# Placing row maxima without the way through DRAM, one group later, and borrowing maxima from the next work item

## The chip, the cores and the metric

The kernel runs on one core of one Trainium2 chip. The metric is device time in microseconds, the median of several executions. The engines of the core run their own instruction lists side by side and wait for one another through semaphores: TensorE (PE) multiplies, VectorE (DVE) takes maxima and small elementwise work, ScalarE (ACT) does the exponentials, GpSimd (POOL) elementwise work in the background, and SyncE (SP) issues nearly all DMAs.

## The reference, cut to what matters

One transformer block over 2048 rows of 512 columns: layer norm, attention with 32 heads of 16 dimensions over all 2048 keys, output projection and residual, then layer norm, a SiLU MLP of width 1792 and a second residual.

```
qkv = (layernorm(x) @ wqkv) -> q, k, v            # 32 heads, 16 wide
p = softmax(q k^T / 4);  o = p v
h = x + o @ wo
out = h + silu(layernorm(h) @ w1) @ w2
```

## The kernel before, in words

**Items and groups.** Attention is cut into 32 items: 4 blocks of 512 query rows times 8 sets of four heads. An item is cut into 16 groups, one for each 128 keys, so there are 512 groups (`g`); item `i` starts at group 16 `i`. In each group four score products (`scores`, `ps<-qs,ks`, one for each head) are made, ScalarE exponentiates each (`pt`), and two groups later `values` multiplies them with the values (`ps<-pt,va`, eight instructions a group, the last of it on TensorE).

**The maxima.** The softmax's row maxima are found by TensorE ahead of the scores: for each item 64 products (`maximum`, `ps<-ks,qs`: 2 row halves times 2 heads, 4 query tiles of 128 rows and 4 key blocks of 512), each reduced by VectorE (line 309, `mx`). When an item's 64 are there, `finish_max` takes the maximum over the key blocks (on VectorE if urgent, otherwise in six steps on GpSimd) and splits each into two 16-bit parts, `ns`, 128 partitions by 32. These parts have to lie as two more rows of each half of the *query stack* `qs` (partitions 64j + 48 and + 49 of half j), so that the score product subtracts the maximum by itself. No score of an item may run before its rows are there.

**Two ways to place them.** `place_max` turns `ns` on TensorE, copies the result (`mn`) and issues two DMAs `qs<-mn`. `place_far` turns 32 by 32 blocks on VectorE (`mt`, a transpose within VectorE), then issues four DMAs into the DRAM tile `md` one step later, and one step after that two DMAs from `md` into `qs`. A step is a group here. `found_maxima` takes the far way when the item starts more than FAR = 5 groups ahead (8 in an output item), and then waits CALM = 2 steps before the turn; otherwise `place_max` follows some steps later, and that group may hold one maximum fewer. The last item (31) always goes by `place_max`, in two pieces.

**Row halves.** Keys and queries of a head fill 64 of TensorE's 128 rows, so two products on different row halves run side by side, and two on the same half one after the other. The order alternates them. `todo[i, half]` holds the maxima of an item still to do in each half, 32 at first.

**Stages.** Groups 0 to 127 run attention alone, with three or so maxima a group. In items 8, 16 and 24 (`FIRSTS`) the attention output of the 512 rows just done is projected. From group 148, 276 and 404, for 112 groups each (`beside`), the MLP's products run beside attention, as halves too (`ps<-hts,w` and `ps<-w,gates`): six half products, four scores and four maxima a group. `beside_products` writes the order of such a group: even groups take the half products of row half 0 with scores of row half 1 for this group and the next, odd groups the other way round; of the maxima three go to the half of the scores and one to the other. How many maxima stand in the group is said by `maxima(g)`:

```
most = 4 - late_now + (64 + 4 * (g + LEAD) > at["done"])
```

with LEAD = 5: a fifth one, as long as the maxima done are behind the goal. `one_max` takes a maximum of the half asked for from the first item that has any left, and of the other half if that one has none; it turned to the next item only if that item's loads are due (`at["ready"]`) and the item's start is over 12 groups away.

**Queues.** All instructions stay in the order in which the program writes them, each engine its own. `soon(n, f)` puts `f` at the beginning of the n-th step from now. SP's queue holds the loads of keys and queries for the item four ahead (in the groups 6 to 13 of an item), the weights' loads, the small transfers of the softmax denominators, and the placing DMAs above.

Of the kernel before, what the change touches and what calls it, by code (L numbers as in the profile page):

```python
# [12 lines left out]
F16 = mybir.dt.float16  # L13
# [7 lines left out]
P = 128  # L21
# [9 lines left out]
KC = S // P  # L31
# [20 lines left out]
RING = 5  # L52

HEADS = [(0, 1), (0, 0), (1, 1), (1, 0)]
ITEMS = NB * H // 4
# [5 lines left out]
FIRSTS = 8, 16, 24  # L61


WAIT = 2
# [1 line left out]

JOINT = 2
MORE = 3, 3, 3, 3
FAR = 5
CALM = 2  # L70


# [1 line left out]

LOOK = 5

LEAD = 5

BEHIND = 4

# [11 lines left out]
def attention_mlp_kernel(ctx: ExitStack, tc: tile.TileContext, x, wqkv, wo, w1, w2, out):  # L92
    nc = tc.nc
    x = x.flatten_outer_dims()
# [14 lines left out]
    def pin(ins):  # L109
        tc.keep_in_program_order(ins)  # L110
# [11 lines left out]
    def dve(fn, *a, **k):  # L122
        pin(getattr(nc.vector, fn)(*a, **k))  # L123
# [4 lines left out]
    def dma(*a):  # L128
        pin(nc.sync.dma_start(*a))
# [27 lines left out]
    dram = ctx.enter_context(tc.tile_pool(name="dram", bufs=1, space=DRAM))  # L157
# [10 lines left out]
    def next_bank(kind):  # L168
        ring = banks[kind]
        ring.append(ring.pop(0))  # L170
        return ring[-1]
# [45 lines left out]
    dn = dram.tile([H, 4, 512], F32, name="dn")  # L217
    dr = dram.tile([H, 4, 512], F32, name="dr")

    md = dram.tile([ITEMS, 32, P], F16, name="md")  # L220

    wd = {kind: dram.tile([FC, P, 2, 512], F16, name=f"{kind}d") for kind in ("w1", "w2")}

    def statistics(rows, scale=1.0):
# [24 lines left out]
    ks, qs = [None] * RING, [None] * RING  # L249
# [26 lines left out]
    def head(g, k):  # L276

        i, c = divmod(g, KC)
        if i < LAST:
            return *HEADS[k], c  # L280
        return c // HALF, k % 2, c % HALF * 2 + k // 2
# [5 lines left out]
    def start_of(piece):  # L287
        i, a = piece
        return KC * i + HALF * (a or 0)

    mx, left = {}, {}
# [24 lines left out]
    def finish_max(piece, urgent):  # L316

        m4 = mx.pop(piece).rearrange("p j a q k -> p (j a q) k")
        rows = m4.shape[1]
        nm = small.tile([P, 16], F32, name="nm")[:, :rows]  # L320
        sign = 1.0
        if urgent:
            pin(nc.vector.tensor_reduce(nm, m4, axis=AX.X, op=ALU.max, negate=True))
        else:
            sign = -1.0
            m1, m2 = m4[:, :, :2], m4[:, :, 2:]
            for to, a, b in ((m2, m1, m2), (nm, m2[:, :, 0], m2[:, :, 1])):

                pool("tensor_tensor", to, b, a, ALU.subtract)
                pool("tensor_scalar", to, to, 0.0, None, op0=ALU.max)  # L330
                pool("tensor_tensor", to, to, a, ALU.add)
        ns = small.tile([P, 32], F16, name="ns")[:, :2 * rows]
        high, rest = (ns.rearrange("p (j r a) -> p j r a", j=2, r=2)[:, :, r, :] for r in range(2))
        nm = nm.rearrange("p (j a) -> p j a", j=2)
        pool("tensor_scalar", nm, nm, sign / MX, None, op0=ALU.mult)
        pool("tensor_copy", high, nm)
        pool("tensor_tensor", rest, nm, high, ALU.subtract)
        split[piece] = ns
# [7 lines left out]
    def place_far(piece):  # L346

        i, _ = piece
        mt = small.tile([P, 32], F16, name="mt")
        dve("transpose", mt, split.pop(piece))  # L350

        def out():
            for b in range(4):
                dma(md[i, :, 32 * b:32 * b + 32], mt[32 * b:32 * b + 32, :])

        def back():
            for j in range(2):
                dma(qs[i % RING][64 * j + 48:64 * j + 50].rearrange("r a n -> r (a n)"),
                    md[i, 16 * j:16 * j + 16, :].rearrange("(r q) n -> r (q n)", r=2))
            placed.add(piece)  # L360

        if at["attention"]:
            soon(1, out)
            soon(2, back)
        else:
            out()
            back()

    def place_max(piece):

# [8 lines left out]
        def out():  # L379
            for j in range(2):  # L380
# [8 lines left out]
    todo = {(i, j): sorted(((i, kb, qt, a, j) for kb in range(4) for a in range(2) for qt in range(4)),  # L389
                           key=lambda t: (t[1], t[3]) if i < 2 else t[3])  # L390
            for i in range(ITEMS) for j in range(2)}
    END = 64 * ITEMS
    at = {"item": 0, "done": 0, "half": 0, "step": 0, "due": 0, "attention": False, "group": None, "ready": 0, "next": 0, "blocks": True}
    agenda, late = {}, {}

    def soon(steps, fn, *a):

        agenda.setdefault(at["step"] + steps, []).append((fn, a))
# [11 lines left out]
    def next_item():  # L410
        while at["item"] < ITEMS and not (todo[at["item"], 0] or todo[at["item"], 1]):
            at["item"] += 1
        return at["item"]

    def found_maxima(piece):
        g = at["group"]
        output = g is not None and g // KC in FIRSTS
        if g is None or piece[1] is None and start_of(piece) - g > FAR + 3 * output:
            soon(WAIT + 1 if g is None else CALM, place_far, piece)
            finish_max(piece, g is not None and g > FIRSTS[0] * KC)  # L420
            return
        late.setdefault(at["step"] + (1 if output else WAIT), []).append(piece)
        unfinished.append(piece)
        found_at["step"] = at["step"]

    def one_max(half=None, n=None):

        i = next_item()
        if i == ITEMS:
            return  # L430
        if half is None:
            half = at["half"]
            at["half"] = 1 - half
        if at["blocks"]:

            i = min(range(2), key=lambda n: (todo[n, half] or todo[n, 1 - half] or [(n, KC)])[0][1])
        elif not todo[i, half] and 64 * (i + 2) <= at["ready"] and KC * i - at["next"] > 12:

            i += 1
        half = half if todo[i, half] else 1 - half  # L440
        maximum(*todo[i, half].pop(0), next_bank("sm") if n is None else n)
# [23 lines left out]
    def singles(n):  # L465
        for _ in range(n):
            one_max()
# [298 lines left out]
    for b in range(NB):  # L766
# [7 lines left out]
        for n, (kind, k) in enumerate(units + vs if b else units):  # L774
# [3 lines left out]
            if b + 1 < NB:  # L778
                rows = xts[b + 1]
# [76 lines left out]
    for g in range(1, NG // 2):  # L856
        for m, (b, key) in enumerate([(b, 1) for b in range(NB)] + [(b, 0) for b in range(NB)]):
# [3 lines left out]
            n = 8 * g + m - 12  # L861
# [340 lines left out]
    def beside_products(g, n):  # L1202

        if not current:
            count, share, of, end = chains.pop(0)
            current.update(count=count, share=share, of=of, end=end, half=[0, 0], open=[], gone=0)
        side = g % 2
        heads = [(x, k) for x in (g - side, g - side + 1) for k in range(4) if head(x, k)[1] != side]
        i, found, left = next_item(), [0, 0], [0, 0]
        if i < ITEMS:  # L1210
            left = [len(todo[i, j]) for j in range(2)]
        count = current["count"] - current["half"][0] if side == 0 else current["half"][0] - current["half"][1]
        count = min(current["share"], count)
        for _ in range(min(n, sum(left))):
            j = 1 - side
            if 4 + found[j] > count + found[side] or found[j] == left[j]:
                j = side
            if found[j] == left[j]:
                j = 1 - j
            found[j] += 1  # L1220
        other = [("score", of) for of in heads]
        for m in range(found[1 - side]):
            other.insert(2 * m if m < 3 else len(other), ("max", 1 - side))
        same = [("half", side)] * count + [("max", side)] * found[side]
        last = max(m for m, step in enumerate(other) if step[0] == "score")
        if last < count - 1:
            other[last:last] = [("none", 0)] * (count - 1 - last)
        for m in range(max(len(other), len(same))):
            for kind, x in same[m:m + 1] + other[m:m + 1]:
                if kind == "score":  # L1230
                    weigh = scores(*x)
                    if current.get("fence", True) is None:
                        current["fence"] = weigh()
                    else:
                        weigh()
                elif kind == "max":
                    one_max(x)
                elif kind == "half":
                    half_product(x)
                    if m == count - 1:  # L1240
                        current["fence"] = None
                        if current["half"][1] == current["count"]:
                            current["end"](space[:, 3, :])
                            current.clear()
# [132 lines left out]
    def maxima(g):  # L1377
# [4 lines left out]
        if g in beside:  # L1382
            at["due"] = 0
            most = 4 - late_now + (64 + 4 * (g + LEAD) > at["done"])
            return max(0, min(most, ready - at["done"]))
# [22 lines left out]
    for g in range(groups):  # L1408
        tick()
        i, c = divmod(g, KC)  # L1410
# [15 lines left out]
        if i in FIRSTS:  # L1426
            b, n = i // 8 - 1, c - OUTPUT
# [23 lines left out]
        n = maxima(g)  # L1451
# [3 lines left out]
        else:  # L1455
            half = 1 - head(g, g % 2)[1]
            j = next_item()
# [59 lines left out]
```

## Time and profile before

| | us |
|---|---|
| median of 3 runs | 1571.74 (1571.65 to 1571.79) |
| the profiled execution | 1571.37 |
| its span, from the first instruction to the last | 1569.6 |
| TensorE busy | 1553.5 |
| VectorE busy | 1377.7 |
| ScalarE busy | 1233.6 |
| GpSimd busy | 552.7 |

The granted TensorE clock was 1.000 over the span. In rows of the profile "a<-b,c" says that tile a is written from b and c; "x8" is the count of instructions merged into a row; the first number of a timeline row is its start after the span's start in us, the second the time it took. "SPq" is an issue of a DMA on SP's queue: the time is that of the issue, not of the transfer.

### The profile page before, as it was taken

What the parts mean: (1) busy time and instruction counts of PE and PEld (TensorE: products, weight loads), DVE (VectorE), ACT (ScalarE), POOL (GpSimd) and SP (SyncE); (2) the same over time, 40 slices, a digit from 0 to 9 for tenths busy, and PEclk for the clock granted to TensorE, in tenths of its full rate; (3) what the DMA queues carried; (4) which work ended last, traced back from release to release, by engine and by line L of the source; (5) the groups of instructions that cost most, each with busy time, mean ns of one, the idle gap of its engine ahead of it and who ended that gap; (6) DMA issues with size and microseconds to landing.
All of it is one profiled execution on the core that took longest, in us unless ns stands there. A gap on an engine that the chain in (4) does not pass through costs nothing.

```text
span 1569.6 us, 31094 instructions
## 1 busy us (share of the span) xinstructions
PE 1553.5 (99%) x11484; PEld 501.1 (32%) x11484; DVE 1377.7 (88%) x2216; ACT 1233.6 (79%) x2404; POOL 552.7 (35%) x759
## 2 busy tenths in 40 slices
PE   9999999999999999999999999999999999999999
PEld 6433322222222333333322333333322333332354
DVE  7999999999999999999999999999999999993322
ACT  6545799999977889888768998888868889888532
POOL 6643544445532344311142444311142544211100
PEclk9999999999999999999999999999999999999999
DMA  6667523333334022345423112444432221335332
GB/s 218 172 173 228 141 78 101 90 108 94 118 86 100 20 61 61 89 137 145 141 71 92 43 44 60 123 142 128 124 93 70 58 56 49 94 106 164 103 88 74
DMA packets 136209, 162.50 MB, mean 104 GB/s; under 512 B 43152, under 2 KB 80080, under 8 KB 136056
## 3 DMA queue, kind: packets, MB, share of 16 engines
q1 hardware_dynamic: 131304, 151.99, 34.8%
q10 hardware_dynamic: 4752, 8.52, 2.0%
q8 instruction: 90, 1.47, 0.4%
q14 instruction: 63, 0.52, 0.1%
HBM read 126.70 MB, written 24.85 MB: 97 GB/s over the span
## 4 chain that ended last, share of the span: by engine, by line
PE 87%; DVE 9%; ACT 2%; issue 1%; POOL 0%; DMA 0%; POOLq 0%; ACTq 0%; DVEq 0%
PE ps L99 87%; DVE mx L309 6%; ACT pt L113 2%; DVE mx L307 1%; PE ps L102 1%; DVE st L123 0%; DVE w L123 0%; DVE pvs L123 0%; DVE ot L123 0%; DVE ks L123 0%; POOL wv_l L106 0%; DMA ks<-in_A_x_dram 0%; POOL rs L106 0%; ACT g L113 0%; DVE mv L123 0%
## 5 line engine op out<-in xcount | busy, mean ns | idle before, releaser
L309 DVE TENSOR_REDUCE mx<-ps 128x1 f32<-128x512 f32 x1842 | 1145.7, 682 | 61.5 <-PE ps L99 31.5
L113 ACT ACTIVATE pt<-ps 128x512 f32<-128x512 f32 x2048 | 1050.0, 607 | 187.0 <-PE ps L99 185.2
L99 PE MATMUL ps<-ks,qs 48*128 48x512 f16 x2048 | 672.0, 379 | 5.7 <-DVE mx L309 2.7
L99 PE MATMUL ps<-qs,ks 64*128 64x512 f16 x2048 | 639.7, 377 | 1.8 <-ACT pt L113 1.4
L99 PE MATMUL ps<-pt,va 128*17 128x512 f32 x4096 | 538.6, 598 | 0.6
L99 PE MATMUL ps<-hts,w 64*128 64x512 f16 (+2 forms) x1212 | 285.0, 372 | 1.8 <-ACT pt L113 1.8
L99 PE MATMUL ps<-w,gates 64*128 64x512 f16 x1008 | 245.6, 378 | 0.1
L99 PEld LDWEIGHTS <-ks 64*128 64x128 f16 x2048 | 177.0, 94 | 212.1 <-issue 169.2
L99 PEld LDWEIGHTS <-qs 48*128 48x128 f16 x2048 | 167.0, 94 | 70.9 <-issue 29.4
L99 PEld LDWEIGHTS <-w 64*128 64x128 f16 (+1 forms) x1212 | 101.9, 95 | 236.8 <-ACT pt L113 107.2
L106 POOL TENSOR_TENSOR ri<-rc,minus 128x16 f32<-128x16 f32 x31 | 90.7, 2926 | 240.0 <-DMA rc<-dn 240.0
L99 PEld LDWEIGHTS <-gates 64*128 64x128 f16 (+1 forms) x1152 | 95.1, 94 | 240.3 <-ACT pt L113 112.8
L99 PEld LDWEIGHTS ps<-pt,va 128*17 128x17 f32 x4096 | 68.2, 95 | 204.9 <-issue 197.0
L307 DVE TENSOR_REDUCE mx<-ps 128x2 f32<-128x1024 f32 x103 | 119.3, 1218 | 4.0 <-PE ps L99 3.5
L106 POOL TENSOR_SCALAR t<-t,factors 128x512 f32<-128x512 f32 x42 | 29.0, 692 | 214.8 <-ACT t L113 214.8
L113 ACT ACTIVATE g<-ps,factors 128x512 f32<-128x512 f32 x68 | 46.9, 690 | 42.7 <-PE ps L99 42.7
L106 POOL TENSOR_TENSOR ot<-ot,g 128x512 f32<-128x512 f32 x12 | 15.3, 1271 | 128.5 <-ACT g L113 128.5
L113 ACT ACTIVATE ks<-ps 128x512 f32<-128x512 f32 x30 | 17.9, 597 | 51.7 <-PE ps L99 46.3
L123 DVE SCALAR_TENSOR_TENSOR gh<-g,factors,gh 128x512 f16<-128x512 f32 x14 | 10.5, 752 | 52.1 <-ACT gh L113 52.1
L106 POOL TENSOR_TENSOR t<-t,g 128x512 f32<-128x512 f32 x42 | 53.7, 1279 | 3.5
L106 POOL TENSOR_TENSOR sl<-ks,sh 128x512 f16<-128x512 f32 x30 | 34.7, 1156 | 50.4 <-ACT sh L113 38.6
L106 POOL TENSOR_TENSOR gates<-t,gates 128x512 f16<-128x512 f32 x42 | 48.6, 1158 | 3.4
(160 smaller groups left out, 992.4 us busy)
## 6 DMA issues: line engine op xcount, KB each, us to landing
w<-w2d SPq DMA_DIRECT2D x182, 256.0 KB
ks<-kd SPq DMA_DIRECT2D x120, 192.0 KB
w<-w1d SPq DMA_DIRECT2D x56, 256.0 KB
ks<-in_B_w_dram ACTq DMA_DIRECT2D x28, 256.0 KB
w<-in_B_w_dram SPq DMA_DIRECT2D x28, 256.0 KB
qs<-qd SPq DMA_DIRECT2D x128, 48.0 KB
kd<-sh SPq DMA_DIRECT2D x16, 256.0 KB
qd<-sh SPq DMA_DIRECT2D x16, 256.0 KB
```

What stands on the lines that cost most here:

```text
L99: return tc.keep_in_program_order(nc.tensor.matmul(*a, **k))
L102: tc.keep_in_program_order(nc.tensor.transpose(*a))
L106: tc.keep_in_program_order(getattr(nc.gpsimd, op)(*a, **k))
L113: ins = getattr(nc.scalar, fn)(*a, **k)
L123: pin(getattr(nc.vector, fn)(*a, **k))
L307: pin(nc.vector.tensor_reduce(of, space[:, n:n + 2, :], axis=AX.X, op=ALU.max))
L309: pin(nc.vector.tensor_reduce(of[:, j:j + 1], space[:, n, :], axis=AX.X, op=ALU.max))
```

## The change

`place_far` no longer writes `mt` to DRAM and back: eight DMAs (four blocks times two halves) go from `mt` straight into the rows of `qs`, one step after the turn. The DRAM tile `md` is gone. FAR falls from 5 to 3, LEAD from 5 to 4, and in groups up to 128 the turn waits three steps in place of two. In the groups beside the MLP, `beside_products` counts the next item's maxima as well if they are ready, and `one_max` may take them (`borrow`) where the first item has none left in the half asked for.

```diff
-FAR = 5
+FAR = 3
...
-LEAD = 5
+LEAD = 4
...
-    md = dram.tile([ITEMS, 32, P], F16, name="md")
...
         def out():
-            for b in range(4):
-                dma(md[i, :, 32 * b:32 * b + 32], mt[32 * b:32 * b + 32, :])
-
-        def back():
             for j in range(2):
-                dma(qs[i % RING][64 * j + 48:64 * j + 50].rearrange("r a n -> r (a n)"),
-                    md[i, 16 * j:16 * j + 16, :].rearrange("(r q) n -> r (q n)", r=2))
+                rows = qs[i % RING][64 * j + 48:64 * j + 50].rearrange("r a (q b n) -> r (a q) b n", b=4, n=32)
+                for b in range(4):
+                    dma(rows[:, :, b, :], mt[32 * b + 16 * j:32 * b + 16 * j + 16, :])
             placed.add(piece)
 
         if at["attention"]:
             soon(1, out)
-            soon(2, back)
         else:
             out()
-            back()
...
-            soon(WAIT + 1 if g is None else CALM, place_far, piece)
+            soon(WAIT + 1 if g is None else CALM if g > FIRSTS[0] * KC else CALM + 1, place_far, piece)
...
-    def one_max(half=None, n=None):
+    def one_max(half=None, n=None, borrow=False):
...
-        elif not todo[i, half] and 64 * (i + 2) <= at["ready"] and KC * i - at["next"] > 12:
+        elif not todo[i, half] and 64 * (i + 2) <= at["ready"] and (borrow or KC * i - at["next"] > 12):
...
-            left = [len(todo[i, j]) for j in range(2)]
+            known = [i, i + 1] if 64 * (i + 2) <= at["ready"] else [i]
+            left = [sum(len(todo[m, j]) for m in known) for j in range(2)]
...
-                    one_max(x)
+                    one_max(x, borrow=True)
```

## The prediction

> **What bounds the kernel now.** I read the page first: the busy shares, the granted clock and the chain that ended last.
>
> ```profile
> span 1569.6 us, 31094 instructions
> ...
> PE 1553.5 (99%) x11484; PEld 501.1 (32%) x11484; DVE 1377.7 (88%) x2216; ACT 1233.6 (79%) x2404; POOL 552.7 (35%) x759
> ...
> PEclk9999999999999999999999999999999999999999
> ...
> PE 87%; DVE 9%; ACT 2%; issue 1%; POOL 0%; DMA 0%; POOLq 0%; ACTq 0%; DVEq 0%
> ```
>
> TensorE is busy 99% of the span at full clock and carries 87% of the chain; VectorE carries 9%. So a change gains where it shortens TensorE's own order or one of the stretches in which VectorE leads, and any idle stretch put into TensorE's order is lost in full: it has no slack to win it back.
>
> Next, TensorE's timeline. Each group ends in eight value products, one row "x8"; from one such row to the next is one group.
>
> ```profile
> 511.07 1.05 PE L99 MATMUL ps<-pt,va 128*17 128x512 f32 x8
> 514.16 1.05 PE L99 MATMUL ps<-pt,va 128*17 128x512 f32 x8
> 517.37 1.05 PE L99 MATMUL ps<-pt,va 128*17 128x512 f32 x8
> 520.17 1.06 PE L99 MATMUL ps<-pt,va 128*17 128x512 f32 x8
> 523.26 1.05 PE L99 MATMUL ps<-pt,va 128*17 128x512 f32 x8
> ...
> 553.03 1.05 PE L99 MATMUL ps<-pt,va 128*17 128x512 f32 x8
> 556.06 1.05 PE L99 MATMUL ps<-pt,va 128*17 128x512 f32 x8
> 558.87 1.05 PE L99 MATMUL ps<-pt,va 128*17 128x512 f32 x8
> 561.48 1.05 PE L99 MATMUL ps<-pt,va 128*17 128x512 f32 x8
> 564.09 1.05 PE L99 MATMUL ps<-pt,va 128*17 128x512 f32 x8
> ```
>
> Beside the MLP a steady group takes 2.61 us (561.48 to 564.09). The exceptions are what the change is about. The first five rows end the groups 154 to 158 and show that five maxima in a group instead of four make it 3.09 us (155, from 511.07 to 514.16); the chain there is VectorE's.
>
> ```profile
> 509.43 3.08 DVE mx L309 x5
> ```
>
> The group that ends with the row at 556.06 (170) takes 3.03 us and the next 2.81, with four maxima each.
>
> **The change, part by part.** I number groups by the scores they belong to (item = group / 16) and followed the planner's rules from group to group; under the old rules they give in each group the count of maxima that the trace shows.
>
> *Lead of four.* A group beside the MLP gets a fifth maximum while done < 64 + 4 (g + LEAD). Before group 148, 664 are done; the old goal there is 676, the new one 672. Each five-group wins one, so the old catch-up is 12 fives (148 to 160, but for 157, where the late rows cost one maximum), the new one eight (148 to 155). Groups 156, 158, 159 and 160 fall from five to four: 156 from 3.21 us (514.16 to 517.37) to about 2.8, VectorE still finishing its backlog, the others from 3.09 to 2.61. Item 10 is found in group 155, five ahead of its start at 160; that now is "far", so the turn on TensorE in 157 goes (2.80, from 517.37 to 520.17, to about 2.65). Together -2.0 us. In the second and third stretch the deficit at entry is five under either rule (both ends moved by four): no gain. The four maxima put off land in group 491, which has none now:
>
> ```profile
> 1417.14 1.05 PE L99 MATMUL ps<-pt,va 128*17 128x512 f32 x8
> 1419.95 1.05 PE L99 MATMUL ps<-pt,va 128*17 128x512 f32 x8
> 1422.55 1.05 PE L99 MATMUL ps<-pt,va 128*17 128x512 f32 x8
> ```
>
> Group 490 with four takes 2.81, 491 without 2.60: +0.2 us.
>
> *Borrowing from the next item.* Halves run in pairs. In group 170 the item has one maximum left for half 1 and three for half 0, where the order wants three and one, so equal halves follow each other unpaired:
>
> ```profile
> 554.88 0.59 PE L99 MATMUL ps<-hts,w 64*128 64x512 f16 x2
> 555.31 0.37 PE L99 MATMUL ps<-qs,ks 64*128 64x512 f16 x1
> 555.32 0.81 PE L99 MATMUL ps<-ks,qs 48*128 48x512 f16 x3
> ```
>
> That is (3.03 - 2.61) + (2.81 - 2.61) = 0.62 us, and the counting gives one such pair of groups in each of the three stretches (170, 282, 410; in the first, the new catch-up leaves no such remnant either). The missing half is now taken from the next item: -1.8 us. The price: in stretches two and three, five groups of 4:1 in turn leave the halves three apart, and the old lack evened this out. Borrowing keeps it: in group 283 only maxima of half 0 are left of item 18, three are taken, one of half 1 comes from item 19, and the last of item 18 comes at the end of 284, four groups ahead of its start at 288. The same holds for items 18 to 24 and 26 to 30: **twelve items complete four ahead** (six before). Items 11 to 16 complete five ahead.
>
> *One group later in the first part.* There GpSimd finishes the maxima and VectorE's turn waits for it:
>
> ```profile
> DVE mt L123 <- POOL ns L106: 2.6, 4, 1.0
> ```
>
> VectorE then is what TensorE waits for:
>
> ```profile
> 294.85 1.05 PE L99 MATMUL ps<-pt,va 128*17 128x512 f32 x8
> 297.80 1.05 PE L99 MATMUL ps<-pt,va 128*17 128x512 f32 x8
> 299.76 1.05 PE L99 MATMUL ps<-pt,va 128*17 128x512 f32 x8
> ```
>
> 2.95 us where a group takes 1.96. The turn one group (1.96 us) later finds its rows finished, since the longest wait was under 1 us: all of it goes, -2.6 us.
>
> *Straight to the stacks.* Before, six issues on SP: four of 32 pieces of 64 bytes to DRAM, and, after they landed, two back. Item 11:
>
> ```profile
> 560.20 0.20 DVE L123 STREAM_TRANSPOSE mt<-ns 128x32 f16<-128x32 f16 x1
> ...
> 560.43 1.69 SPq L129 DMA_DIRECT2D md<-mt  x4
> 562.16 0.43 SPq L129 DMA_DIRECT2D ks<-kd  x1
> 563.29 0.52 SPq L129 DMA_DIRECT2D qs<-md  x2
> ...
> 570.57 0.38 PE L99 MATMUL ps<-qs,ks 64*128 64x512 f16 x1
> ```
>
> The turn stands 0.28 us into group 172 (559.92, the end of the x8 row at 558.87), SP issues at once, the back copies are issued by 563.81, and item 11's first score runs at 570.57: over 5 us of cover. Now there are eight issues, all from SBUF to SBUF, 16 pieces of 64 bytes each, two partitions as target. What does such an issue cost on SP? Not traced; two bounds. From below the copies out of the same tile, 1.69 us for four, 0.42 each (0.46 from one to the next when they follow at median length). From above the other writers of those two rows, also SBUF to SBUF and in 16 pieces:
>
> ```profile
> L129 SPq DMA_DIRECT2D qs<-mn x12: 616/647/717, 476.5 to 1426.3; - x12
> ...
> 476.50 1.41 SPq L129 DMA_DIRECT2D qs<-mn  x2
> ```
>
> 0.65 us each, 1.41 for two. The target and piece count are theirs, so I take 0.70 us from issue to issue: eight make 5.6. Landing: 562.12 to 563.29, 1.17 us, the least; the most by
>
> ```profile
> 907.59 1.69 SPq L129 DMA_DIRECT2D md<-mt  x4
> 909.33 1.56 SPq L129 DMA_DIRECT2D ks<-kd  x1
> 912.03 0.52 SPq L129 DMA_DIRECT2D qs<-md  x2
> ```
>
> is 2.75 (909.28 to 912.03). I take 1.2, as the copies no longer write DRAM.
>
> The deadline of an item found four ahead: the turn is placed two groups after, at start - 2, done 0.48 us into it; the copies stand in SP's order one group later but SP is idle by then, as at 560.43. First score in its group: the second pair (570.34 and 570.57 in item 11), so two groups and 0.21, 5.43 us (two groups back is 565.14). That score is of row half 1, whose four copies are issued last. Rows are there at 0.5 + 5.6 + 1.2 = 7.3. **TensorE stands still for about 1.8 us at the start of each of the twelve items: +21.6 us.** Found five ahead, the deadline is 8.08: no stall, 0.8 to spare. Behind the copies on SP wait weight loads, which run groups ahead: nothing.
>
> Item 8, in the first part, is found in 121; with the extra group its copies also come behind one more load of SP's:
>
> ```profile
> 424.16 1.05 PE L99 MATMUL ps<-pt,va 128*17 128x512 f32 x8
> ...
> 426.52 0.41 SPq L129 DMA_DIRECT2D ks<-kd  x1
> 427.03 1.76 SPq L129 DMA_DIRECT2D md<-mt  x4
> 428.83 0.42 SPq L129 DMA_DIRECT2D qs<-qd  x1
> ```
>
> From 427.5, after that load: 427.5 + 5.6 + 1.2 = 434.3. Group 124 begins at 425.21; without VectorE's wait four groups of 1.96 end at 433.05, and the first score is of half 1: +1.2 us. Items 3 to 7 have twelve groups or more.
>
> **Sum:** -2.0 + 0.2 - 1.8 - 2.6 + 21.6 + 1.2 = +16.6. The profiled execution took 1571.37 us, 0.37 under the median shown; 1571.74 + 16.6 = 1588.3, rounded to 1588.
>
> The Trainium skill (DMA: Bandwidth & Descriptors, "Issuing engines are not separate DMA queues") says that the time a sequencer needs to start a DMA is usually small beside the DMA itself. By that rule, eight issues would cost little and the sum would be that of the first rival; the rows of qs<-mn and md<-mt speak against it, since two issues of 4 KB in all hold SP for 1.41 us and the landing behind them is of the same size.
>
> **Rivals.** *The issues are cheap* (the other side). At md<-mt's 0.46 us the rows land at 0.5 + 3.7 + 1.2 = 5.4, just in time: no stall, and item 8's goes too. 1571.74 - 6.2 = 1565.5. For it: same source tile, same piece of 64 bytes. Against: every SBUF-to-SBUF issue into those rows takes over 0.6. The sign turns at (0.52 + 5.43 - 1.7) / 8 = 0.53 us an issue, where twelve stalls of 0.52 us eat the 6.2.
>
> *The items complete five ahead after all*, because borrowing is held back by the loads that are ready, or halves even out. Then only item 8 waits: 1571.74 - 6.2 + 1.2 = 1566.7. Against: the next item's keys are loaded four items ahead, so nothing holds it back.
>
> *The copies land late*, 2.75 us as at 912.03: the stall is 3.4 us, twelve make 41, six five-ahead items wait 0.7 each, 4.2, and item 8 waits 2.8: 1571.74 + 41 + 4.2 - 6.2 + 2.8 = 1613.5. For it: one of the traced chains; against: the landing there was a write to DRAM beside a 192 KB load, and in the last two groups before an item no such load is issued.
>
> **Chances and range.** The forecast 0.70 (by itself 1581 to 1598: the issue 0.64 to 0.75, from the shortest and the longest qs<-mn and some 0.03 between two, the landing 1.1 to 1.5 in the mean); cheap issues 0.17; five ahead 0.06; late landing 0.07. The range takes in the first two rivals: 1565 to 1598. Within 0.2% (3.1 us), about what a measurement of this kernel can tell from no change, is 1568.6 to 1574.9: an issue near the turning point, 0.05, taken from cheap issues and the forecast. Faster 0.20, same 0.05, slower 0.75.
>
> **What will show it.** The row of qs<-mt: x216 or so, 600 ns or more each, eight in a row over 5 us. Waits of TensorE or its weight loads on a DMA qs<-mt, about 13 times and near 1.8 us; idle stretches at the starts of items 18 to 24 and 26 to 30, none at 11 to 16. The wait of mt on POOL gone; no fives after group 155; no 3.03 at 170, 282 and 410. An issue of qs<-mt under 0.5 us, or no TensorE wait on it, makes the prediction wrong.

## The result: 0.7% slower, and the profile after

| | before | changed |
|---|---|---|
| median, us | 1571.76 (1571.65 to 1571.90) | 1583.09 (1582.93 to 1583.44) |
| the profiled execution, us | 1571.37 | 1582.93 |
| its span, us | 1569.6 | 1581.1 |

The ratio is 1.0073, with a 95% interval of 1.0061 to 1.0085. The page after, busy shares and chain:

```profile
span 1581.1 us, 31233 instructions
...
PE 1552.2 (98%) x11483; PEld 500.1 (32%) x11483; DVE 1379.8 (87%) x2216; ACT 1233.4 (78%) x2404; POOL 554.1 (35%) x759
...
PE 74%; DVE 13%; SPq 4%; DMA 4%; ACT 2%; issue 2%; POOL 1%; DVEq 0%; POOLq 0%; ACTq 0%
```

TensorE's busy time fell by 1.3 us while the span grew by 11.5: the added time is idle, not work. New in the chain are SP's queue and DMAs, 4% each. A share of the chain is not a cost: SP's copies run beside TensorE's products for most of their time, and only the part that outlasts them lengthens the span (below). One item's beginning in the chain after, in order of time (item 21, start at group 336; the reductions `mx` are line 309 before and line 307 in this kernel):

```profile
994.82 0.22 issue
995.04 0.68 DVE mx L307
995.72 0.12 DVE mt L123
995.84 0.68 DVE mx L307
996.52 0.04 SPq L129
996.55 0.05 issue
996.61 0.66 SPq L129
997.27 0.05 issue
997.32 0.61 SPq L129
...
999.94 0.61 SPq L129
1000.55 0.04 issue
1000.59 1.63 DMA qs<-mt
1002.22 0.14 issue
1002.36 7.71 PE ps L99 x60
```

VectorE's turn is followed by SP issuing one copy after another, the last copy's issue and landing, and then TensorE. The same item in the timelines of SP and TensorE:

```profile
994.37 1.05 PE L99 MATMUL ps<-pt,va 128*17 128x512 f32 x8
...
995.87 5.33 SPq L129 DMA_DIRECT2D qs<-mt  x8
...
1000.62 0.39 PE L99 MATMUL ps<-w,gates 64*128 64x512 f16 x1
1000.62 0.39 PE L99 MATMUL ps<-ks,qs 48*128 48x512 f16 x1
1000.85 0.38 PE L99 MATMUL ps<-w,gates 64*128 64x512 f16 x1
1002.36 0.37 PE L99 MATMUL ps<-qs,ks 64*128 64x512 f16 x1 [1.14 <-DMA qs<-mt]
```

The group before last begins at 995.42, where the x8 row ends, and the copies 0.45 us into it. The first pair of the item's first group runs at 1000.62. The score belongs to the second, at 1000.85, and starts 1.51 us after that, when the eighth copy has landed: its issue ended at 1001.20, the chain puts the landing at 1002.22, and the score starts at 1002.36, 1.16 after the issue's end. The bracket, 1.14, is TensorE's idle time alone; before it the partner product at 1000.85 ran without the score beside it. The group is 1.50 us longer than before.

The ends of the value products also show how far ahead VectorE's turn stands: in the kernel before in the fourth group ahead of an item's start for items 11 to 16 and for the twelve items, in the changed kernel in the third for items 11 to 16 and in the second for the twelve.

The costs and gains of all groups, from the ends of their value products in the two profiles:

| where | predicted, us | measured, us |
|---|---|---|
| starts of items 18 to 24 and 26 to 30, twelve stalls | +21.6 | +17.3 (1.37 to 1.50 each) |
| start of item 8 | +1.2 | +0.9 |
| groups 39, 60, 103, 124 | -2.6 | -2.6 |
| first stretch, groups 153 to 164 | -2.0 | -2.1 |
| unmatched pairs, groups 170, 171, 282, 283, 410, 411 | -1.8 | -1.7 |
| end of the maxima, groups 484 to 494 | +0.2 | +0.2 |
| all groups | +16.6 | +11.8 |

The span grew by 11.5 and not 11.8, since what follows the last value product is 0.2 us shorter.

The waits of the changed kernel and the row of the tile behind them:

```profile
PE ps L99 <- DMA qs<-mt: 13.7, 13, 1.1
PEld L99 <- DMA qs<-mt: 10.2, 7, 1.7
```
```profile
L129 SPq DMA_DIRECT2D qs<-mt x224: 596/610/742, 117.9 to 1400.9; - x112
L123 DVE STREAM_TRANSPOSE mt<-ns x28: 200/202/202, 115.0 to 1395.9; 128x32 f16<-128x32 f16 x28
its engine sat idle before it (us, times) until:
who waited for it (us, times):
```

The 13 waits of the first line are the twelve items and item 8. VectorE's wait of 2.6 us for ns is gone (nothing stands under "until"), and TensorE's long groups with it; in the timeline after, the group that was 2.95 us has the length of its neighbours:

```profile
294.52 1.05 PE L99 MATMUL ps<-pt,va 128*17 128x512 f32 x8
296.48 1.05 PE L99 MATMUL ps<-pt,va 128*17 128x512 f32 x8
```

### The profile page after: what moved, and what is told of

The parts are those of the page before. It is cut to its first block, busy times and chain, and to the rows that moved or that the text cites. A ratio compares the mean times of both kernels' runs of the same rounds, so it can differ in the third digit from the quotient of the medians.

```text
span 1581.1 us, 31233 instructions
## 1 busy us (share of the span) xinstructions
PE 1552.2 (98%) x11483; PEld 500.1 (32%) x11483; DVE 1379.8 (87%) x2216; ACT 1233.4 (78%) x2404; POOL 554.1 (35%) x759
## 4 chain that ended last, share of the span: by engine, by line
PE 74%; DVE 13%; SPq 4%; DMA 4%; ACT 2%; issue 2%; POOL 1%; DVEq 0%; POOLq 0%; ACTq 0%
PE ps L99 74%; DVE mx L307 9%; SPq L129 4%; ACT pt L113 2%; DMA qs<-mt 1%; DVE mx L305 1%; DMA w<-w2d 1%; DVE st L123 1%; PE ps L102 0%; DVE w L123 0%; DMA va<-in_A_wqkv_dram 0%; DMA hts<-gates 0%; DMA ks<-in_A_x_dram 0%; DVE pvs L123 0%; DMA ks<-kd 0%
## 5 line engine op out<-in xcount | busy, mean ns | idle before, releaser
L106 POOL TENSOR_SCALAR nm<-nm 128x16 f32<-128x16 f32 (+1 forms) x42 | 10.8, 258 | 147.2 <-DVE nm L321 141.8
```

Source lines behind the costliest of these rows:

```text
L106: tc.keep_in_program_order(getattr(nc.gpsimd, op)(*a, **k))
```

## The experiments

The theory: the rows are late because SP issues eight copies one after the other, the first score needs the last four of them, and borrowing leaves only two groups for it. The rivals: copies from SBUF to SBUF or their landing are slow by themselves, whatever their order; a lead of four is too short by any way; something else in the change costs time.

### Half 1 first

```diff
-            for j in range(2):
+            for j in (1, 0):
```

> The changed kernel with the eight copies in another order: the four of row half 1 first, then those of half 0. Theory (SP's serial issue): the first score of an item belongs to half 1, and what makes it late is that its four copies stand fifth to eighth in a row of issues of 0.655 us. First in the row they land at 0.5 + 4 x 0.655 + 1.2 = 4.3 us after the group before last has begun, before the score's 5.43; half 0 is due one group (2.61 us) later at 8.0 and lands at 6.9. The twelve stalls of 1.45 us go: 1583.1 - 17.4 = 1565.7 us; item 8's wait of 0.9 stays, since there half 0 follows at once. Rival (the copies themselves, or their landing, are slow from SBUF to SBUF, or the lead of four is too short by any order): the stall stays or falls by under half, 1575 us or more.

Measured: 1565.58 us (1565.40 to 1566.19); ratio to before 0.9961 (0.9948 to 0.9975), so faster than both kernels. The same item in this kernel's timelines of VectorE, SP and TensorE:

```profile
991.17 0.20 DVE L123 STREAM_TRANSPOSE mt<-ns 128x32 f16<-128x32 f16 x1
...
991.40 5.33 SPq L129 DMA_DIRECT2D qs<-mt  x8
...
996.16 0.39 PE L99 MATMUL ps<-w,gates 64*128 64x512 f16 x1
996.16 0.39 PE L99 MATMUL ps<-ks,qs 48*128 48x512 f16 x1
996.39 0.38 PE L99 MATMUL ps<-w,gates 64*128 64x512 f16 x1
996.39 0.38 PE L99 MATMUL ps<-qs,ks 64*128 64x512 f16 x1
```

SP is held just as long, 5.33 us, and still issuing when the group begins at 996.16; the score at 996.39 does not wait, since its half is there. The eight issues are as slow as before and cost nothing now. All twelve stalls are gone; item 8 still waits, as there half 0 follows at once, but its first group is 0.64 us longer than before and not 0.9, as the expectation had it.

### One place earlier

```diff
-            for j in range(2):
+            for j, b in ((0, 0), (0, 1), (0, 2), (1, 0), (1, 1), (1, 2), (1, 3), (0, 3)):
                 rows = ...
-                for b in range(4):
-                    dma(rows[:, :, b, :], ...)
+                dma(rows[:, :, b, :], ...)
```

> The changed kernel with one copy of half 0 moved behind those of half 1, so that the last one the first score needs is the seventh in the row and not the eighth. Theory (serial issue): each place in the row is worth one issue, so the stall falls from 1.45 to 0.80 us in twelve items, and item 8's, which needs both halves at once, stays: 1583.1 - 12 x 0.655 = 1575.2 us. Rival (the time from the last issue to the landing is what is too long, whichever place): no change, 1583 us.

Measured: 1575.10 us (1574.71 to 1575.62), ratio 1.0021 (1.0012 to 1.0030). The twelve groups are 0.71 to 0.84 us longer than before the change, in place of 1.37 to 1.50: one place is one issue, 0.65 us. The time is set by the place in SP's row of issues. Item 8 did not quite stay: its first group is 0.66 longer than before, in place of 0.89.

### A lead of five

```diff
-LEAD = 4
+LEAD = 5
```

> The changed kernel with LEAD at 5 again, all else as changed (direct copies, half 0 first, borrowing). By the planner's rules all items then complete five groups ahead. Theory: the rows land at 7.1 us and are due at 8.0, so no item but the eighth waits: minus 12 x 1.45; four groups of the first stretch (156 to 159) hold five maxima again, plus 4 x 0.46: 1583.1 - 17.4 + 1.8 = 1567.5 us. Rival (borrowing or the direct copies cost something that doesn't hang on the lead): over 1571 us.

Measured: 1568.14 us (1567.96 to 1568.64), ratio 0.9978 (0.9969 to 0.9987); expected 1567.5. None of the twelve items waits. The five-groups of the first stretch are back (156 to 159, 3.1 to 3.2 us), and group 490 is 0.43 us longer than before: in TensorE's timeline its 15 half products, scores and maxima stand in ten places one after another, in eight before, so more of them run without a partner. The expectation left this cost out.

### The way through DRAM kept

The copies of the kernel before (`out` and `back` over `md`), all else as changed.

```diff
+            for b in range(4):
+                dma(md[i, :, 32 * b:32 * b + 32], mt[32 * b:32 * b + 32, :])
+
+        def back():
             for j in range(2):
-                rows = ...
...
+                dma(qs[i % RING][64 * j + 48:64 * j + 50].rearrange("r a n -> r (a n)"),
...
+            soon(2, back)
```

> The changed kernel with the rows going through DRAM as before (four issues out of 0.42 us, after their landing two back of 0.24), LEAD 4, FAR 3, borrowing and the later turn kept: twelve items still complete four ahead. Theory (serial issue): 0.5 + 1.7 + 1.2 + 0.5 + 1.2 = 5.1 us, just before the 5.43, so the way through DRAM with its two landings is the quicker one here: stalls of 0 to 0.5 us, 1565 to 1569 us. Rival (a lead of four is too short by any way): stalls as in the changed kernel, about 1583 us.

Measured: 1567.61 us (1567.00 to 1568.15), ratio 0.9974 (0.9964 to 0.9984). With the same lead, the way with two landings is 15.5 us faster than the direct one. Nine of the twelve items don't wait at all; three do, by 0.33, 0.73 and 1.35 us. The longest, on SP and TensorE:

```profile
1254.78 1.69 SPq L129 DMA_DIRECT2D md<-mt  x4
1259.34 0.52 SPq L129 DMA_DIRECT2D qs<-md  x2
```
```profile
1261.13 0.37 PE L99 MATMUL ps<-qs,ks 64*128 64x512 f16 x1 [0.98 <-DMA qs<-md]
```

From 1256.47 to 1259.34 SP waited 2.87 us for the landing in DRAM, where the other eleven items took 1.0 to 1.2. In the two other items that wait (20 and 24) it was the four issues out of `mt` that took longer, 2.5 and 3.0 us in place of 1.69. So a lead of four is enough by this way, and by the direct one with half 1 first, but the way through DRAM has no margin for a slow issue or landing.

### Without borrowing

```diff
-            known = [i, i + 1] if 64 * (i + 2) <= at["ready"] else [i]
+            known = [i]
...
-                    one_max(x, borrow=True)
+                    one_max(x)
```

> The changed kernel without borrowing (one_max and beside_products look at the first item alone again), LEAD 4 and the direct copies with half 0 first kept. By the planner's rules the last maxima of an item are then taken from the half that has some left, so all items complete five ahead, and two groups (283 and 411) hold one pair less well matched. Theory (borrowing lets the halves drift, an item ends one group later, and only that makes the rows late): the twelve stalls go, plus 2 x 0.2 us: 1583.1 - 17.5 + 0.4 = 1566.0 us. Rival (lateness comes from the lead of four itself): 1583 us or more, as the unmatched pairs come back as well.

Measured: 1566.14 us (1566.08 to 1566.41), ratio 0.9965 (0.9951 to 0.9978). No item of the twelve waits, and VectorE's turn stands in the third group ahead of their starts again; groups 283 and 411 are 0.22 us longer than with borrowing. Borrowing, added to the lead of four, thus brought 0.4 us and, through the later ends of the items, cost 17.3.

### The later turn alone

```diff
-            soon(WAIT + 1 if g is None else CALM, place_far, piece)
+            soon(WAIT + 1 if g is None else CALM if g > FIRSTS[0] * KC else CALM + 1, place_far, piece)
```

> The kernel before with one line of the change: in groups up to 128 VectorE's turn waits three steps in place of two. Theory: VectorE no longer waits for GpSimd, the four long groups (39, 60, 103, 124) fall to 1.96 us, minus 2.6, and item 8 may wait 0.3: 1569.3 us. Rival (those waits were hidden, the gain of the whole change outside the stalls lies in the lead and the borrowing alone): 1571.7 us.

Measured: 1569.48 us (1568.91 to 1569.85), ratio 0.9985 (0.9976 to 0.9994). The four groups fall to 1.96 us, together -2.63, and item 8's first group is 0.39 longer.

### The direct copies alone

In the kernel before, only `place_far`'s copies are those of the change.

```diff
-                dma(md[i, :, 32 * b:32 * b + 32], mt[32 * b:32 * b + 32, :])
...
+                    dma(rows[:, :, b, :], mt[32 * b + 16 * j:32 * b + 16 * j + 16, :])
```

> The kernel before with the direct copies alone (half 0 first; FAR 5, LEAD 5, no borrowing, turn after two steps). All far items complete six ahead, so the rows land at 7.1 us where they are due at 10.6. Theory: where there is that much cover the route costs and saves nothing: 1571.7 us, within 0.5. Rival (the SBUF-to-SBUF copies hold up other work on SP or the DMA engines): 1573 us or more.

Measured: 1571.79 us (1571.58 to 1572.18), ratio 1.0001 (0.9992 to 1.0010). With items six ahead, the eight slow issues on SP make no item wait and the shorter way saves nothing; one group, 475, is 0.28 us longer (see below).

### Two more edits

On the kernel with half 1 first:

```diff
-        if at["attention"]:
+        if at["attention"] and at["next"] > FIRSTS[0] * KC:
             soon(1, out)
...
-        if g is None or piece[1] is None and start_of(piece) - g > FAR + 3 * output:
+        if g is None or piece[1] is None and start_of(piece) - g > FAR:
```

> The changed kernel with half 1 first, and two more edits: up to group 128 the copies are issued in the step of the turn, and items 9, 17 and 25, found in output items, go by VectorE and the direct copies too (no three groups added to FAR). Theory: item 8's copies pass one load on SP and its wait falls from 0.64 by 0.47; the two or three turns on TensorE with their missing maximum go, 0.2 us each: 1564.5 us. Rival (SP is held in the output items by the transposing DMAs, so that the rows of those three items are late): 1567 us or more.

Measured: 1573.00 us (1572.62 to 1573.63), ratio 1.0008 (0.9999 to 1.0017), 7.4 us behind the kernel with half 1 first; 1564.5 was expected. Group 128 did fall by 0.31 us (0.47 expected), but item 9's first group takes 10.25 us in place of 3.23, which is nearly the whole loss. VectorE, SP and TensorE there:

```profile
475.43 0.20 DVE L123 STREAM_TRANSPOSE mt<-ns 128x32 f16<-128x32 f16 x1
```
```profile
476.57 2.96 SPq L133 DMA_TRANSPOSE hts<-gates  x2
479.58 5.33 SPq L129 DMA_DIRECT2D qs<-mt  x8
```
```profile
483.44 0.37 PE L99 MATMUL ps<-qs,ks 64*128 64x512 f16 x1 [4.41 <-DMA qs<-mt]
483.44 0.39 PE L99 MATMUL ps<-ks,qs 48*128 48x512 f16 x1
486.00 0.58 PE L99 MATMUL ps<-qs,ks 64*128 64x512 f16 x1 [2.17 <-DMA qs<-mt]
```

The turn is done at 475.63, but the copies stand behind two transposing DMAs on SP and begin 3.95 us later. Four of them are issued by 482.2, and the score of half 1 starts 1.2 us after that, at 483.44; the last is issued by 484.91, and the score of half 0 starts at 486.00: the same sum of issues and landing, met twice in one item. The rival held for item 9 only: item 17 waits 0.47 us for its rows, which stand behind no transposing DMA, and item 25 does not wait for them.

## Why the prediction was right, and where its sizes were off

The step that decided was named: eight SBUF-to-SBUF issues at the price of qs<-mn, the last four for the first score, for twelve items four ahead because of borrowing. The first experiment shows the order, the second the price of a place, the fifth the part of borrowing, the third and seventh that more cover removes it. That the time lies in 1565 to 1598 says little by itself, since this range holds a kernel that is faster as well as one that is slower; the thirteen waits at the items named, and the traced issues of `qs<-mt`, are what bears the prediction out.

The stall was put at about 1.8 us (the terms give 1.87) and is 1.44 in the mean. In item 21 it is 0.45 + 5.33 + 1.16 - 5.43 = 1.51 us: the start was put at 0.5, the eight issues at 5.6 and the landing at 1.2. So 0.27 of the 0.36 us lies in the issue time, which is the term that was mis-sized: 0.70 from one issue to the next, where the trace has 0.74 and 0.71 for the first two and 0.65 for the rest. Over the twelve items the stalls were put 4.3 us too high. Item 8 came out at 0.9, not 1.2; its issues took 5.27 us and the landing 1.06. The nearest row, `qs<-mn`, was the right choice, but its copies are larger: 4 KB each for that item, not "4 KB in all" for the two, against 1 KB of `qs<-mt`.

The gains were right to 0.2 us each, since each was the length of a group in the trace before. One of them had the wrong cause, though: the -1.8 us of the unmatched pairs were put down to borrowing. Without borrowing 1.3 of the 1.7 us remain (fifth experiment), and with borrowing and a lead of five all of it is there (third), so the lead of four brings most of it by itself, and borrowing on top of it 0.4 us. That items five ahead do not wait was right as well: none of 11 to 16 does.

The Trainium skill's rule that a sequencer's time to start a DMA is usually small beside the DMA itself (DMA: Bandwidth & Descriptors, "Issuing engines are not separate DMA queues") does not hold for these copies: of the 1.63 us from the start of the eighth copy's issue to its landing the issue takes 0.61, and eight of them hold SP for 5.33 us.

Of the rivals, cheap issues did not come, as the row of qs<-mt shows (596 ns the shortest). The twelve items came five ahead only where borrowing was taken out or the lead raised to five. A late landing was not seen for the direct copies in the twelve items, but was for the way through DRAM, at 2.87 us.

What stays open: group 475 is 0.28 us longer in the changed kernel and in each profile compared for it with direct copies (2.93 us against 2.65), and not with the way through DRAM. ScalarE begins its first exponential there 0.27 us later, and the last score follows it; what holds ScalarE the profile does not show, and no run was made for it.

## What to carry to other kernels

When a transfer on a deadline is cut into many small DMAs on one queue, count issues times the issue time of the nearest traced form, and ask which of them the first reader needs: putting those first turned a loss of 11 us into a gain of 6 here, with not one instruction less. A shorter way (no DRAM, one landing less) can be the later one. And a planner's rule that fills gaps by taking work of the next item also moves the end of the present one: look up what hangs on that end.

## What the runs showed that was not expected

In the last kernel TensorE ran only two products (0.39 us) between 479.03 and 486.00, and the granted clock fell to half and came back. The stretches with TensorE's busy time and, in the column PEclk, the clock:

```profile
core 0: us, PE busy (x) PEld busy (x) DVE busy (x) ACT busy (x) POOL busy (x), PEclk, DMA share, GB/s
482.00:483.00 1.00, 0.00 (x0) 0.00 (x0) 0.00 (x0) 0.00 (x0) 0.00 (x0) 1.00 0.02 2
483.00:484.00 1.00, 0.39 (x2) 0.13 (x2) 0.12 (x1) 0.15 (x1) 0.00 (x0) 0.87 0.01 1
484.00:485.00 1.00, 0.00 (x0) 0.00 (x0) 0.57 (x1) 0.45 (x1) 0.00 (x0) 0.50 0.02 2
489.00:490.00 1.00, 1.00 (x8) 0.28 (x6) 0.11 (x1) 0.15 (x1) 0.00 (x0) 0.50 0.00 0
490.00:491.00 1.00, 1.00 (x9) 0.28 (x9) 1.00 (x2) 1.00 (x3) 0.00 (x0) 0.72 0.00 0
491.00:492.00 1.00, 1.00 (x10) 0.11 (x4) 0.78 (x2) 0.98 (x3) 0.00 (x0) 1.00 0.00 0
```

From the shares 0.87 and 0.72 the clock was at half from about 483.7 to 490.6. It fell before the second idle stretch began, so the first, of 4.41 us, was enough, while the changed kernel's twelve of 1.0 to 1.1 us left it at 1.000 over the span. It came back 4.6 us after the products had begun again at 486.00. The Trainium skill says that the clock is halved after a window of about 3.4 us without work and restored after about as long a busy one (TensorE: Matmul & The Clock Gate, "What's actually happening"); both observations agree with it. At half clock a group's eight value products took 1.91 us in place of 1.05. So a late transfer costs its wait and, when the wait is long enough (more than 1.1 us, at most 4.41 by these runs), some microseconds of slow products behind it.
